# Row order for the later batches' scores, and the second batch's loads queued behind the second weight quarter

## The chip, the cores and the metric

One core of one Trainium2 chip runs the whole program. The metric is the device time of one execution in microseconds (us). Before the change it is 761.84 us, the median of 3 runs (760.61 to 761.95).

## The reference

Four batches (B) of 576 rows (S) go through attention with 8 heads (H) of 64 numbers (D), whose keys and values are first condensed to 32 memory slots (M), and then through two feed-forward layers of 512 and 2048 columns. Everything is float32.

```python
a = softmax(phi, axis=sequence)                      # b h s m
k_m, v_m = a.T @ k, a.T @ v                          # b h 32 64
attn = softmax(q @ k_m.T / 8, axis=memory) @ v_m     # b h 576 64
x = attn.transpose(0, 2, 1, 3).reshape(2304, 512)
x = lrelu(x @ w_in) @ w_out                          # first layer, slope 0.01
h = x @ w_in2
out = (h * tanh(softplus(h))) @ w_out2               # second layer, result 2304 x 512
```

## The kernel before, in words

The kernel has one TensorE (PE), VectorE (DVE) and ScalarE (ACT), and one queue (SP) that issues every DMA in program order. Attention and the first layer are joined: with `win` (a quarter of `w_in`, 512 columns) the condensed values are multiplied ahead (`vw_tasks`, L923: the product at L943, then a high and a low part of it in 32-bit rounded form by `hi_lo`, L317), so that a row of softmax weights (`at_t`) times `vw_t` gives the hidden layer (`stage1`, L1182: product at L1193, evictions at L1207, difference at L1214, second product with `wo_t` at L1226). The work of `stage1` comes in items of one batch, one half of its 576 rows (288 columns of the moving operand) and one 128-column block `m` of the hidden layer. The first 16 items are those of batch 0: 8 with the first quarter of `w_in`, 8 with the second; then follows batch 1. The weights come as bit patterns of float64 and are decoded by ACT and DVE (`load_raw`, L342; `decode`, L359); the first two quarters go through seven raw buffers, `raw_t` (3) and `raws_t` (4).

For batches 1 to 3, `kv_rest` (L502) loads phi, k and v and condenses them (fold at L522, PE at L533, L557, L597, the condensing product at L620, transposes at L651 to L663), and `score_rest` (L674) loads q, transposes it in 32 x 32 blocks on DVE (L691), so that a partition holds one number of a head's 32 and the free dimension holds (r, e, i) for row 18 i + r and half e of the 64, and multiplies it with the keys on PE (L709), in two halves of the rows. A half has 2 x 4 x 2 products; each stands in the trace as two PE instructions, so a half is 32. Softmax follows on DVE and ACT (L720 to L752). Half `hf` takes the rows with r from 9 hf to 9 hf + 8, and its 288 columns stand in the order (r, i).

Two other lines that the prediction uses: the reductions of phi in batch 0 (L450) read it in steps of 32 elements, where those of the scores (L729) read neighbours; batch 0's copies of the transposed q (L840, recorded as L310) write it in steps of 9 elements.

The second layer works on blocks of 768 rows. Its last products (`chunk`, L1617: product L1701, evictions at L1729 and L1736) end in result tiles of 128 rows and 256 columns, which `fo` (L1743) stores. Because of the order of the columns, a result tile's 128 partitions are rows at one distance (2) only in batch 0, whose q goes another way (`score_tasks`, L807); in the later batches they are 4 (or 3, 2, 1) groups of 32 rows, each row 18 from the next.

The order on each engine is written by a planner (`Order.run`, L94) when the program is built. Every task has a due time (`prio`), costs and dependencies; among those ready by the planner's own clock the earliest due is issued. The loads of batch 1 are due by `pl` and `pq`; the second half of its scores by `S1` after the first. Buffers come from small rings; two PSUM tiles `misc_t` serve L533 to L663, L709 and L943 in turn.

Of the kernel before, what the change touches and what calls it, by code (L numbers as in the profile page):

```python
# [23 lines left out]
def hop(a, b):  # L24
# [4 lines left out]


K = dict(
    LAG1=2, WIN=8, OB=2, RS=4, FILL=36, A1=10, S1=2.8,
    A2=30, S2=2.6, V1=2.4, V2=14, W2=56.0, W2S=3.8, O='phi0 kv0 phi1 q0 w0 kv1 q1 w1 w2 w3', HF0=-20.0, HF1=-7.0,
    HFD=0.3, TOP=0.3, HI=0.2, WO=2.0, WOL=1, WC=3.0, WC0=-38.0, V0=3.0, COLD=20, GL=1.5, AL=5.0, XL=22.0, T='0:1 0:1 1:2 0:2 1:2', SB=1,
    DW=280e3, DQ=1.3, DP=1.2, DS=0.78, DI=0.38, L4=0.5, L4P=1.6, L4S=0.8, L4T=5.0, MA=6, QL=4, FK=-52.5, DWF=0.85, MV="......rvvrrvvrvr",
)


# [35 lines left out]
class Task:  # L74
    def __init__(self, engines, prio, fn, deps, take, use, bias):
        self.engines, self.prio, self.fn, self.take = engines, prio, fn, take
        self.deps = [d for d in deps if d is not None]
        self.after, self.end, self.bias = [], None, bias
        for b in list(take) + list(use):
            b.users.append(self)  # L80


class Order:
# [10 lines left out]
    def run(self, window):  # L94
        n_wait, ready = {}, []
        for i, t in enumerate(self.tasks):
            t.n = i
            t.deps = list({id(d): d for d in t.deps + [d for b in t.take for d in b.res.after]}.values())
            n_wait[i] = len(t.deps)
            for d in t.deps:  # L100
                d.after.append(t)
            if not t.deps:
                t.at = dict.fromkeys(t.engines, 0.0)
                ready.append(t)
        free = {"PE": 1.7, "ACT": 1.5, "DVE": 0.5, "POOL": 0.8, "SP": 0.0}
        events = []
        now, dma_free, left, main = 0.0, 1.68, len(self.tasks), -1.0
        while left:
            ready.sort(key=lambda t: (t.prio, t.n))
            hit = False  # L110
            for t in list(ready):
                if t.prio > main + window and t.take:
                    continue
                start = {e: max(now, free[e], t.at[e]) for e in t.engines}
                eng = min(start, key=lambda e: start[e] + t.engines[e] + t.bias.get(e, 0))
                if start[eng] > now + 1e-9:
                    continue
                got = []
                for b in t.take:
                    if not b.res.can_take(b, now, eng):  # L120
                        break
                    b.res.take(b)
                    got.append(b)
                if len(got) < len(t.take):
                    for b in got:
                        b.res.undo()
                    continue
                t.eng, t.st0 = eng, now
                self.issued = 0
                t.fn(eng)  # L130
                if eng == "SP":
                    free[eng] = now + K["DI"] * self.issued
                    dma_free = max(dma_free, now + 0.6) + t.engines[eng]
                    t.end = dma_free + 1.8
                else:
                    free[eng] = t.end = now + t.engines[eng]
                main = max(main, getattr(t, "main", -1.0))
                ready.remove(t)
                left -= 1
                hit = True  # L140
                for a in t.after:
                    n_wait[a.n] -= 1
                    if not n_wait[a.n]:
                        a.at = {e: max(d.end + hop(d.eng, e) for d in a.deps) for e in a.engines}
                        ready.append(a)
                        for x in a.at.values():
                            heapq.heappush(events, x)
                for e in free:
                    heapq.heappush(events, t.end + hop(eng, e))
                heapq.heappush(events, free[eng])  # L150
            if not hit:
                while events and events[0] <= now:
                    heapq.heappop(events)
                assert events, [(t.prio, t.fn.__qualname__) for t in ready[:12]]
                now = events[0]
        return now
# [3 lines left out]
def kernel(  # L160
# [341 lines left out]
    def kv_rest(b, p0, dp):  # L502
        ph = tags["phi"].new([P, HG, RB, M])
        kv = [kvq.new([P, 2, 2, RB, D]) for _ in range(NG)]
        pl = p0 - 6
        pairs = lambda x: x[b].rearrange("(x e) (t j) d -> (e t) x j d", e=2, j=RB)
        l_phi = load(pl, ph.make, lambda: pairs(phi), 589824, (), [ph], (), K["DS"])

# [1 line left out]
        for g in range(NG):  # L510

            def ld(e, g=g):
                kv[g].make()
                for j, x in enumerate((k, v)):
                    dma(out=kv[g].t[:, j], in_=pairs(x)[:, 2 * g:2 * g + 2])

            l_kv.append(add({"SP": K["DS"] * mb(1179648)}, pl + 0.2 + 0.1 * g, ld, (), [kv[g]]))

        def fold(buf, op, last):
            xs = ph.t.rearrange("p x j m -> p j x m")  # L520
# [153 lines left out]
    def score_rest(b, pq, ps, dp):  # L674
# [3 lines left out]
        for g in range(NG):  # L678
            flat = lambda g=g: q_of[g]().rearrange("p r e i -> p (r e i)")
            new = b == 1 or not g  # L680

            def ld(e, g=g, new=new, flat=flat):
                if new:
                    qs[g].make()
                dma(out=flat(), in_=q[b, g * HG:(g + 1) * HG].rearrange("h (p r) d -> (h p) (r d)", r=RQ))

            ld0 = add(
                {"SP": K["DS"] * mb(589824)}, pq - K["QL"], ld, [] if new else [ld0], [qs[g]] if new else [], [] if new else [qs[g]],
            )
            parts.append(add(  # L690
                {"DVE": dve(1152) + 0.1}, pq + 0.7 * g, lambda e, flat=flat: nc.vector.transpose(out=flat(), in_=flat()), [ld0], (), [qs[g]],  # L691
            ))
# [3 lines left out]
        for hf in range(2):  # L696
# [4 lines left out]
            def fsc(e, hf=hf, T=T, pss=pss):  # L701
                T.make()
                for x in pss:
                    x.make()
                for y in range(2):
                    for h in range(HG):
                        for g in range(NG):
                            rows, o = slice(M * h, M * (h + 1)), M * (h ^ g)
                            nc.tensor.matmul(  # L709
                                out=pss[g].t[o:o + M, :].rearrange("p (r i) -> p r i", i=M),  # L710
                                lhsT=kb.t[rows, g, y, :],
                                rhs=q_of[g]()[rows, RB * hf:RB * (hf + 1), y, :],
                                start=(y == 0),
                                stop=(y == 1),
                            )
# [202 lines left out]
            [] if hf else [a], [T, a] if hf else [T],  # L918
        )))

    win, win_ready, w_scr = {}, {}, {}

    def vw_tasks(b, c, p0):  # L923

# [70 lines left out]
    def w_chunk(c):  # L995
        p = at_item["1", 0, 0, 4 * c] - K["WC"] if c else K["WC0"]
        for g in range(NG):
            wb = win_tag.new([P, 2, 512])
            win[0, c, g] = wb
            ready = []  # L1000
            for j in range(2):
                b, ld = load_raw(p - K["WOL"] + 0.1 * j if c else PW[2 * g + j], "w", 2 * g + j, c, raws if c < 2 else rawm)
                ready.append(
                    decode(
                        p + 0.1 * (2 * g + j), b, ld, (lambda wb=wb, j=j: wb.t[:, j]),
                        ready[:1], [wb] if j == 0 else [], [] if j == 0 else [wb],
                    )
                )
            win_ready[0, c, g] = ready

            def f(e, c=c, g=g, wb=wb):
                d = dram.tile([P, 2, 512], F32, name=f"wscr{c}{g}")
                w_scr[c, g][0] = d
                dma(out=d, in_=wb.t)

            w_scr[c, g] = [None, None]
            w_scr[c, g][1] = add({"SP": mb(524288)}, p + 3, f, ready, (), [wb])
# [580 lines left out]

    out_v = out.rearrange("(b p r) f -> b r p f", b=B, r=2)
    out_b = [out_v[x // 2, x % 2] for x in range(2 * B)]  # L1600
    out_j = [out[x // 2 * S:(x // 2 + 1) * S].rearrange("(i u j) f -> u j i f", u=2, j=RB)[x % 2] for x in range(2 * B)]
    rows = [(ob_tag.new([P, DM]), 0) for _ in range(2)]
    for j in range(2):
        xo = x1_tag.slots[j].new([P, 2 * S])
# [12 lines left out]
    def chunk(c):  # L1617
# [10 lines left out]
        for k7, (nm, a, tn, way) in enumerate(PROD):  # L1628
# [91 lines left out]
            for t in range(NT):  # L1720
# [20 lines left out]
                if half2 and nm in ("P4", "P5", "P2", "P3"):  # L1741

                    def fo(e, g=g, t=t, k2=k2, ob=ob):  # L1743
                        x = (2 * s + g) * NB2 + t * P
                        end = x + P
                        while x < end:
                            hf, p0 = divmod(x, NB1)
                            n = min(NB1 - p0, end - x)
                            o = x - (end - P)
                            cs = slice(k2 * 256, (k2 + 1) * 256)  # L1750
                            if hf < 2:
                                dma(out=out_b[hf][p0:p0 + n, cs], in_=ob.ap()[o:o + n, :])
                            else:
                                dma(out=out_j[hf][p0 // M:(p0 + n) // M, :, cs], in_=ob.ap()[o:o + n, :])
                            x += n

                    add({"SP": mb(P * 1024)}, pe_p + 0.1, fo, [ev], (), [ob])
# [55 lines left out]
```

## Time and profile before

| | us |
|---|---|
| median of 3 runs | 761.84 |
| the profiled execution | 761.22 |
| its span | 759.3 |
| PE busy in the span | 733.2 (97%) |
| DVE busy | 545.0 (72%) |
| ACT busy | 404.0 (53%) |

The chain of waits that ended last is PE for 92% of the span, and its two largest lines are L1226 (27%) and L1547 (21%). PE's granted clock is 0.99 of full speed as a mean. Rows in a profile name line, engine, operation and output<-inputs; "x" is a count, and "idle before" is the time for which the engine stood still ahead of an instruction, with what released it. Where many instructions of PE run side by side, their durations overlap, so a stretch's length says more than their sum.

### The profile page before, as it was taken

The page shows a single profiled execution, that of the slowest core. Times are in us where ns is not written, and L with a number is a line of the kernel's source. Part 1 is how long each engine was busy: PE and PEld are TensorE (multiplying, and loading weights), DVE is VectorE, ACT ScalarE, POOL GpSimd, SP SyncE. Part 2 cuts the span into 40 slices and gives each one's busy share as a digit, 9 for nine tenths or more (in the row PEclk, how much of TensorE's full clock was granted, in tenths as well). Part 3 has the DMA queues.
Part 4 walks back from the last instruction along what each step waited for, and adds up shares of the span by engine and source line. Part 5 has one row for each costly group of instructions (what it writes and reads, how often), then busy time and mean ns, then how long its engine had stood idle before and what let it go on. Part 6 is the DMA issues. An engine that isn't in the chain of part 4 may idle for free.

```text
span 759.3 us, 16148 instructions
## 1 busy us (share of the span) xinstructions
PE 733.2 (97%) x6167; PEld 700.9 (92%) x6167; DVE 545.0 (72%) x1137; ACT 404.0 (53%) x883; POOL 0.7 (0%) x6
## 2 busy tenths in 40 slices
PE   8898999999999999999999999999999999999992
PEld 7685999988998989999999999999999999999992
DVE  6897759787676957465779898675677856656781
ACT  3865449545464556464466656544555644454440
POOL 0000000000000000000000000000000000000000
PEclk9999999999999999999999999999999999999997
DMA  9952955547858397864279888788988788895572
GB/s 349 412 203 85 343 174 185 190 143 267 279 198 328 128 316 270 269 225 149 88 284 380 304 318 264 243 250 283 293 262 252 231 263 257 274 297 165 158 229 70
DMA packets 90274, 183.76 MB, mean 242 GB/s; under 512 B 7510, under 2 KB 42326, under 8 KB 90198
## 3 DMA queue, kind: packets, MB, share of 16 engines
q1 hardware_dynamic: 90198, 182.74, 71.4%
q8 instruction: 48, 0.79, 0.4%
q14 instruction: 28, 0.23, 0.1%
HBM read 140.25 MB, written 42.47 MB: 241 GB/s over the span
## 4 chain that ended last, share of the span: by engine, by line
PE 92%; DVE 2%; DMA 2%; ACT 1%; issue 1%; SPq 0%; DVEq 0%; ACTq 0%
PE acc_t L1226 27%; PE h_t L1547 21%; PE acc_t L1701 16%; PE h_t L1193 13%; PE misc_t L1701 6%; PE acc_t L1547 2%; PE misc_t L943 2%; PE misc_t L620 1%; DMA kvq_t<-in_q_dram 1%; PE acc_t L484 1%; DMA wo_t<-tscr 1%; PE misc_t L709 1%; PE acc_t L1024 1%; PE h_t L833 0%; DVE raws_t L387 0%
## 5 line engine op out<-in xcount | busy, mean ns | idle before, releaser
L1226 PE MATMUL acc_t<-hi_t,wo_t 128*128 128x288 f32 x1024 | 161.5, 298 | 0.4 <-ACT at_t L310 0.3
L1226 PEld LDWEIGHTS acc_t<-hi_t,wo_t 128*128 128x128 f32 x1024 | 143.7, 188 | 10.3 <-issue 4.7
L1701 PE MATMUL acc_t<-wo_t,hi_t 128*128 128x256 f32 x720 | 134.1, 280 | 1.3 <-DMA wo_t<-tscr 1.3
L1193 PE MATMUL h_t<-at_t,vw_t 128*128 128x288 f32 x768 | 124.4, 298 | 2.2 <-ACT at_t L310 0.8
L1701 PEld LDWEIGHTS acc_t<-wo_t,hi_t 128*128 128x128 f32 x720 | 118.1, 188 | 2.1 <-issue 1.0
L1207 ACT ACTIVATE hi_t<-h_t 128x288 fp32r<-128x288 f32 x128 | 52.6, 411 | 119.7 <-PE acc_t L1226 102.9
L1193 PEld LDWEIGHTS h_t<-at_t,vw_t 128*128 128x128 f32 x768 | 110.0, 190 | 3.2 <-ACT at_t L310 1.1
L1701 PE MATMUL acc_t<-wo_t,lo_t 128*128 128x256 f32 x360 | 102.1, 284 | 0.0
L1214 DVE TENSOR_TENSOR lo_t<-e_t,hi_t 128x288 fp32r<-128x288 f32 x128 | 57.2, 450 | 54.0 <-ACT e_t L1207 26.4
L1226 PE MATMUL acc_t<-lo_t,wo_t 128*128 128x288 f32 x512 | 90.6, 299 | 1.4 <-DVE lo_t L1214 1.4
L1226 PEld LDWEIGHTS acc_t<-lo_t,wo_t 128*128 128x128 f32 x512 | 74.6, 188 | 8.7 <-issue 6.2
L1547 PE MATMUL h_t<-xt_t,vw_t 128*128 128x384 f32 x396 | 79.1, 336 | 0.0
L1670 DVE TENSOR_TENSOR lo_t<-wo_t,hi_t 128x384 fp32r<-128x384 f32 x94 | 52.0, 555 | 37.2 <-ACT hi_t L310 35.8
L1547 PE MATMUL h_t<-xt_t,wo_t 128*128 128x384 f32 x352 | 75.5, 336 | 0.0
L1701 PEld LDWEIGHTS acc_t<-wo_t,lo_t 128*128 128x128 f32 x360 | 67.7, 188 | 0.0
L1547 PEld LDWEIGHTS h_t<-xt_t,vw_t 128*128 128x128 f32 x396 | 66.7, 188 | 0.3 <-DVE wo_t L1566 0.3
L310 ACT ACTIVATE hi_t<-wo_t 128x384 fp32r<-128x384 f32 x83 | 43.4, 523 | 41.3 <-PE acc_t L1701 28.8
L1547 PEld LDWEIGHTS h_t<-xt_t,wo_t 128*128 128x128 f32 x352 | 59.5, 188 | 0.1
L1701 PE MATMUL misc_t<-wo_t,hi_t 128*128 128x256 f32 x288 | 54.1, 280 | 0.0
L1207 ACT ACTIVATE e_t<-h_t 128x288 f32<-128x288 f32 x128 | 52.0, 406 | 0.0
L1670 DVE TENSOR_TENSOR lo_t<-vw_t,hi_t 128x384 fp32r<-128x384 f32 x50 | 27.7, 555 | 25.5 <-ACT hi_t L310 25.2
L1572 ACT ACTIVATE wo_t<-wo_t 128x384 f32<-128x384 f32 x53 | 27.6, 520 | 32.4 <-DVE wo_t L1566 32.2
(242 smaller groups left out, 1050.9 us busy)
## 6 DMA issues: line engine op xcount, KB each, us to landing
wo_t<-tscr SPq DMA_DIRECT2D x168, 256.0 KB
vw_t<-wsum SPq DMA_DIRECT2D x32, 512.0 KB
win_t<-wscr SPq DMA_DIRECT2D x24, 512.0 KB
raw_t<-in_moe_w_in_dram SPq DMA_DIRECT2D x19, 512.0 KB
raw_t<-in_moe_w_out_dram SPq DMA_DIRECT2D x17, 512.0 KB
wsum<-vw_t SPq DMA_DIRECT2D x16, 512.0 KB
wo_t<-wsum SPq DMA_DIRECT2D x16, 512.0 KB
tscr<-raw_t SPq DMA_DIRECT2D x9, 512.0 KB
```

The lines of the kernel that those rows point to most:

```text
L310: nc.scalar.activation(out=o, in_=i, func=AF.Copy)
L484: nc.tensor.matmul(out=acc.t[rows, :].rearrange("p (j d) -> p j d", j=2), lhsT=phv()[rows, r, :], rhs=kv.t[rows, :2304].rearrange("p (j r ...
L620: nc.tensor.matmul(out=accs_[g].t[o:o + M, :].rearrange("p (j d) -> p j d", j=2), lhsT=ph.t[rows, x, j, :], rhs=kv[g].t[rows, :, x % 2, j, :],
L943: nc.tensor.matmul(out=pss[g].t[M * (h ^ g):M * (h ^ g) + M, :], lhsT=vT[b, g][0].t[rows, g, h ^ g if b else h // 2, :], rhs=wbs[g].t[rows ...
L1193: nc.tensor.matmul(out=h.t, lhsT=us[g][0].t[:, wi, j0:j0 + P], rhs=ats[g][0].t[:, ai, cols], start=(n == 0), stop=(n == 3 * NG - 1),)
L1207: nc.scalar.activation(out=o, in_=h.t, func=AF.Prelu, alpha=0.01)
L1214: lambda e: nc.vector.tensor_tensor(out=lb.make(), in0=eb.t, in1=hb.t.bitcast(F32), op=ALU.subtract),
L1226: nc.tensor.matmul(out=ac[kk].t, lhsT=wu[0].t[:, wi, kk * P:(kk + 1) * P], rhs=(hb if src == 0 else lb).t, start=(first and (wi, src) == ( ...
L1547: nc.tensor.matmul(out=h.t, lhsT=w[:, wi, c0:c0 + P], rhs=xp[b, xi].ap()[:, j], start=(first and j == 0 and k3 == 0), stop=(j == 1 and k3 ...
L1572: lambda e: nc.scalar.activation(out=t_of[x](), in_=h.t if h else t_of[x](), func=AF.Mish),
L1670: lambda e, hb=hb, lb=lb, src=src: nc.vector.tensor_tensor(out=lb.make(), in0=src(), in1=hb.t.bitcast(F32), op=ALU.subtract),
L1701: nc.tensor.matmul(out=ac[t].t, lhsT=x.t[:, t * P:(t + 1) * P], rhs=T[:, wi], start=(u == 0 and n3 == 0 and first_of), stop=(u == CH - 1 a ...
```

## The change

Four things change. The column order of the scores of batches 1 to 3 becomes (i, r) with r of one parity per half, so that column c of half u is row 2 c + u. For this PE reads q at L709 in steps of 128 elements (512 bytes) instead of one after the other. Second, all result tiles are stored by the one form that batch 0 had, 128 rows at distance 2. Third, a task can name loads that must have been issued ahead of it (`behind`): batch 1's k, v and q wait for the fourth load of the second quarter of `w_in` (index 3 of `w_loads[1]`; index 9 is beyond the list and asks nothing of phi). Fourth, `S1` goes from 2.8 to 8.0, which puts the second half of batch 1's scores later.

```diff
-    LAG1=2, WIN=8, OB=2, RS=4, FILL=36, A1=10, S1=2.8,
+    LAG1=2, WIN=8, OB=2, RS=4, FILL=36, A1=10, S1=8.0,
-    ... MA=6, QL=4, FK=-52.5, ...
+    ... MA=6, QL=4, PL=6, BH=(9,3,3,3,3), FK=-52.5, ...
...
-        self.after, self.end, self.bias = [], None, bias
+        self.after, self.end, self.bias, self.behind = [], None, bias, []
...
-                if t.prio > main + window and t.take:
+                if t.prio > main + window and t.take or any(not hasattr(x, "st0") for x in t.behind):
...
-        pl = p0 - 6
+        pl = p0 - (K["PL"] if b == 1 else 6)
...
+        if b == 1:
+            l_phi.behind, l_kv[0].behind, l_kv[1].behind = [w_loads[1][x:x + 1] for x in K["BH"][:3]]
...
+            if b == 1:
+                ld0.behind = w_loads[1][K["BH"][3 + g]:][:1]
...
-                                out=pss[g].t[o:o + M, :].rearrange("p (r i) -> p r i", i=M),
+                                out=pss[g].t[o:o + M, :].rearrange("p (i r) -> p i r", i=M),
                                 lhsT=kb.t[rows, g, y, :],
-                                rhs=q_of[g]()[rows, RB * hf:RB * (hf + 1), y, :],
+                                rhs=q_of[g]()[rows].rearrange("p (r u) e i -> p u e i r", u=2)[:, hf, y],
...
+                w_loads[c].append(ld)
...
-    out_j = [out[x // 2 * S:(x // 2 + 1) * S].rearrange("(i u j) f -> u j i f", u=2, j=RB)[x % 2] for x in range(2 * B)]
...
-                            if hf < 2:
-                                dma(out=out_b[hf][p0:p0 + n, cs], in_=ob.ap()[o:o + n, :])
-                            else:
-                                dma(out=out_j[hf][p0 // M:(p0 + n) // M, :, cs], in_=ob.ap()[o:o + n, :])
+                            dma(out=out_b[hf][p0:p0 + n, k2 * 256:(k2 + 1) * 256], in_=ob.ap()[o:o + n, :])
```

What the planner makes of it shows at three places. On SP near the start (`wscr` is a quarter of `w_in` written back after decoding, `in_moe_w_in_dram` a load of `w_in`, here of its second quarter), before:

```order
L279 DMA kvq_t<-in_k_dram 128x2x576
L279 DMA kvq_t<-in_v_dram 128x2x576
L279 DMA wscr_369<-win_t 128x1024
L279 DMA raw_t<-in_moe_w_in_dram 128x1024
L279 DMA qs_t<-in_q_dram 128x1152
L279 DMA raw_t<-in_moe_w_in_dram 128x1024
L279 DMA kvq_t<-in_k_dram 128x2x576
L279 DMA kvq_t<-in_v_dram 128x2x576
L279 DMA qT_t<-in_q_dram 128x1152
L279 DMA wscr_458<-win_t 128x1024
L279 DMA raws_t<-in_moe_w_in_dram 128x1024 x2
L279 DMA raws_t<-in_moe_w_out_dram 128x1024 x2
```

And the same place of the changed kernel:

```order
L279 DMA wscr_366<-win_t 128x1024
L279 DMA raw_t<-in_moe_w_in_dram 128x1024 x2
L279 DMA wscr_448<-win_t 128x1024
L279 DMA raws_t<-in_moe_w_in_dram 128x1024 x2
L279 DMA kvq_t<-in_k_dram 128x2x576
L279 DMA kvq_t<-in_v_dram 128x2x576
L279 DMA kvq_t<-in_k_dram 128x2x576
L279 DMA kvq_t<-in_v_dram 128x2x576
L279 DMA qs_t<-in_q_dram 128x1152
L279 DMA qT_t<-in_q_dram 128x1152
L279 DMA raws_t<-in_moe_w_out_dram 128x1024 x2
```

All six loads of batch 1's k, v and q moved behind the four loads of the second quarter. On PE, in batch 0's second half of `stage1`, before:

```order
L1226 MATMUL acc_t<-hi_t,wo_t 128x288 x8
L1226 MATMUL acc_t<-lo_t,wo_t 128x288 x4
L1226 MATMUL acc_t<-hi_t,wo_t 128x288 x8
L1226 MATMUL acc_t<-lo_t,wo_t 128x288 x4
L1226 MATMUL acc_t<-hi_t,wo_t 128x288 x8
L597 MATMUL misc_t<-ones,rm_t 128x1 x2
L1226 MATMUL acc_t<-lo_t,wo_t 128x288 x4
L943 MATMUL misc_t<-win_t,vTb_t 32x512 x8
L620 MATMUL misc_t<-kvq_t,phi_t 32x128 x72
L1193 MATMUL h_t<-at_t,vw_t 128x288 x12
```

In the changed kernel (its L947 is L943 of before, L1231 is L1226, L1198 is L1193, L535 is L533, L559 is L557), some 15 rows earlier:

```order
L1231 MATMUL acc_t<-lo_t,wo_t 128x288 x4
L947 MATMUL misc_t<-win_t,vTb_t 32x512 x8
L1231 MATMUL acc_t<-hi_t,wo_t 128x288 x8
L1198 MATMUL h_t<-at_t,vw_t 128x288 x6
L1231 MATMUL acc_t<-lo_t,wo_t 128x288 x4
L535 MATMUL misc_t<-ident,rm_t 128x128
L1198 MATMUL h_t<-at_t,vw_t 128x288 x6
L1231 MATMUL acc_t<-hi_t,wo_t 128x288 x6
L559 MATMUL misc_t<-rm_t,ones 64x128 x2
L1231 MATMUL acc_t<-hi_t,wo_t 128x288 x2
L1231 MATMUL acc_t<-lo_t,wo_t 128x288 x4
L1231 MATMUL acc_t<-hi_t,wo_t 128x288 x8
```

The product with the second quarter (L943) moved ahead of batch 1's three small PE steps, and `stage1`'s first products go on without a break; L620 stands 20 rows behind L943 now. On SP at the end of the program, a piece of the difference:

```order
-L279 DMA out_dram<-ob_t 4x32x256
-L279 DMA out_dram<-ob_t 2x32x256 x2
-L279 DMA out_dram<-x_t 4x32x256
-L279 DMA out_dram<-ob_t 4x32x256
-L279 DMA out_dram<-ob_t 2x32x256 x2
-L279 DMA out_dram<-x_t 4x32x256
+L279 DMA out_dram<-ob_t 128x256
+L279 DMA out_dram<-ob_t 64x256 x2
+L279 DMA out_dram<-x_t 128x256
+L279 DMA out_dram<-ob_t 128x256
+L279 DMA out_dram<-ob_t 64x256 x2
+L279 DMA out_dram<-x_t 128x256
```

Only the form of the stores changed there, not their number or place. Behind the second half of batch 1's scores the rows of PE are the same in both kernels.

## Rows read from the trace of the kernel before

**Rows 1.** Busy time by stretch: us, PE, PEld, DVE, ACT, POOL, clock, DMA share, GB/s.

```profile
46.00:58.00 12.00, 11.70 (x97) 10.27 (x95) 10.94 (x23) 8.12 (x20) 0.00 (x0) 1.00 0.23 90
58.00:66.00 8.00, 4.82 (x154) 3.78 (x147) 6.19 (x12) 5.02 (x10) 0.00 (x0) 0.79 0.55 188
...
80.00:200.00 120.00, 120.00 (x1124) 110.05 (x1123) 87.72 (x186) 66.11 (x156) 0.00 (x0) 1.00 0.66 229
...
380.00:735.00 355.00, 354.42 (x2509) 353.44 (x2508) 260.76 (x538) 188.90 (x393) 0.00 (x0) 1.00 0.81 264
```

**Rows 2.** Chain that ended last, its end: start, us, what.

```profile
737.81 6.88 DMA wo_t<-tscr
...
746.24 0.35 DVE x_t L1736
```

**Rows 3.** Busy time by stretch, one full stretch and the end.

```profile
536.00:541.00 5.00, 5.00 (x39) 5.00 (x38) 4.12 (x9) 2.18 (x5) 0.00 (x0) 1.00 1.01 337
...
746.00:748.00 2.00, 0.13 (x2) 0.00 (x0) 0.59 (x2) 0.00 (x0) 0.00 (x0) 1.00 0.25 80
...
756.00:758.00 2.00, 0.00 (x0) 0.00 (x0) 0.00 (x0) 0.00 (x0) 0.00 (x0) 0.50 0.12 44
```

**Rows 4.** DMA issues on SP in order of time: start, us.

```profile
536.89 0.34 SPq L279 DMA_DIRECT2D out_dram<-ob_t  x1
...
746.41 3.86 SPq L279 DMA_DIRECT2D out_dram<-ob_t  x3
750.37 1.14 SPq L279 DMA_DIRECT2D out_dram<-x_t  x1
```

**Rows 5.** Waits of SP from 730 us on: us, times, longest.

```profile
SPq L1808 <- DMA out_dram<-ob_t: 5.4, 1, 5.4
...
SPq L1808 <- DMA out_dram<-x_t: 1.3, 1, 1.3
```

**Rows 6.** Waits of PE in the whole span.

```profile
PE misc_t L620 <- DVE vw_t L326: 2.5, 2, 2.4
...
PE acc_t L1701 <- DMA wo_t<-tscr: 1.3, 3, 0.7
```

**Rows 7.** SP and DVE from 31 to 57 us, in order of time.

```profile
31.12 4.54 SPq L279 DMA_DIRECT2D raws_t<-in_moe_w_in_dram  x2
...
34.60 0.68 DVE L326 TENSOR_TENSOR wo_t<-raws_t,wo_t 128x512 fp32r<-128x512 f32 x1
...
56.28 0.68 DVE L387 SCALAR_TENSOR_TENSOR win_t<-raws_t 128x512 int32<-128x512 int32 x1
```

**Rows 8.** L620 from 55 to 70 us, and from 220 to 250 us: busy, mean ns.

```profile
L620 PE MATMUL misc_t<-kvq_t,phi_t 64*32 64x128 f32 x144 | 4.4, 396 | 3.2 <-DVE vw_t L326 2.5 <-issue 0.7
...
L620 PE MATMUL misc_t<-kvq_t,phi_t 64*32 64x128 f32 x144 | 2.2, 271 | 0.0
```

**Rows 9.** SP and DVE at the start, in order of time.

```profile
0.74 0.40 SPq L279 DMA_DIRECT2D phi_t<-in_phi_dram  x1
...
3.78 1.14 DVE L450 TENSOR_REDUCE rm_t<-phi_t 128x32 f32<-128x576 f32 x1 [2.82 <-DMA phi_t<-in_phi_dram]
```

**Rows 10.** Chain that ended last: one half of batch 3's scores.

```profile
245.27 1.13 PE misc_t L709 x32
```

**Rows 11.** PE in order of time: two neighbouring rounds of batch 1's scores.

```profile
69.64 0.40 PE L709 MATMUL misc_t<-qs_t,kT_t 32*32 32x288 f32 x1
...
69.88 0.40 PE L709 MATMUL misc_t<-qs_t,kT_t 32*32 32x288 f32 x1
```

**Rows 12.** DVE and ACT by line and form: busy, mean ns.

```profile
L450 DVE TENSOR_REDUCE rm_t<-phi_t 128x32 f32<-128x576 f32 x4 | 4.5, 1131 | 3.8 <-DMA phi_t<-in_phi_dram 2.8 <-ACT phi_t L466 1.0
L729 DVE TENSOR_REDUCE sm_t<-T_t 128x18 f32<-128x576 f32 x2 | 1.5, 749 | 0.0
...
L310 ACT ACTIVATE kvq_t<-h_t 128x384 f32<-128x384 f32 x2 | 1.7, 861 | 3.6 <-PE h_t L833 3.6
```

**Rows 13.** The page's groups of instructions: busy, mean ns of one.

```profile
L310 ACT ACTIVATE hi_t<-wo_t 128x384 fp32r<-128x384 f32 x83 | 43.4, 523 | 41.3 <-PE acc_t L1701 28.8
```

More of the change, by code (lines that the diff above doesn't have):

```diff
@@ L31 @@
 K = dict(
-    LAG1=2, WIN=8, OB=2, RS=4, FILL=36, A1=10, S1=2.8,
+    LAG1=2, WIN=8, OB=2, RS=4, FILL=36, A1=10, S1=8.0,
     A2=30, S2=2.6, V1=2.4, V2=14, W2=56.0, W2S=3.8, O='phi0 kv0 phi1 q0 w0 kv1 q1 w1 w2 w3', HF0=-20.0, HF1=-7.0,
     HFD=0.3, TOP=0.3, HI=0.2, WO=2.0, WOL=1, WC=3.0, WC0=-38.0, V0=3.0, COLD=20, GL=1.5, AL=5.0, XL=22.0, T='0:1 0:1 1:2 0:2 1:2', SB=1,
-    DW=280e3, DQ=1.3, DP=1.2, DS=0.78, DI=0.38, L4=0.5, L4P=1.6, L4S=0.8, L4T=5.0, MA=6, QL=4, FK=-52.5, DWF=0.85, MV="......rvvrrvvrvr",
+    DW=280e3, DQ=1.3, DP=1.2, DS=0.78, DI=0.38, L4=0.5, L4P=1.6, L4S=0.8, L4T=5.0, MA=6, QL=4, PL=6, BH=(9,3,3,3,3), FK=-52.5, DWF=0.85, MV="......rvvrrvvrvr",
 )
@@ L919, in half @@
         )))
-    win, win_ready, w_scr = {}, {}, {}
+    win, win_ready, w_scr, w_loads = {}, {}, {}, [[] for _ in range(NC)]
     def vw_tasks(b, c, p0):
@@ L1749, in fo @@
                             o = x - (end - P)
-                            cs = slice(k2 * 256, (k2 + 1) * 256)
-                            if hf < 2:
-                                dma(out=out_b[hf][p0:p0 + n, cs], in_=ob.ap()[o:o + n, :])
-                            else:
-                                dma(out=out_j[hf][p0 // M:(p0 + n) // M, :, cs], in_=ob.ap()[o:o + n, :])
+                            dma(out=out_b[hf][p0:p0 + n, k2 * 256:(k2 + 1) * 256], in_=ob.ap()[o:o + n, :])
                             x += n
```

## The prediction

> **What bounds the kernel now.** I read the page's busy times first: PE is the bound. The table of stretches says where it is not full: between 80 and 200 us PE is busy for all of 120 us and from 380 to 735 us for 354.4 of 355, while DVE stands at about 73% [rows 1]. In such a stretch a PE instruction more or less is time more or less, and nothing else is. So I looked for what lies outside: the start, the stretch around 60 us, and the end.
>
> At the end the last additions on DVE finish at 746.24 + 0.35 = 746.6 us [rows 2], but the span ends at 759.3 us, 12.7 us later. In this time no engine works, and the DMA share is 0.25, then 0.12: with 16 DMA engines, 4 and then 2 of them [rows 3]. In the stretch 536 to 541 us, where batch 0's tiles are stored among weight loads, the share was 1.01 at 337 GB/s against 80 and 44 GB/s here [rows 3]. So the last stores are spread over 4 and 2 engines: the 4x32x256 and 2x32x256 forms of the order have an outermost size of 4 and 2. SP has issued its last store at 750.37 + 1.14 = 751.5 us [rows 4], then waits 5.4 and 1.3 us for stores to land [rows 5], which makes 758.2 us; 1.1 us of closing follow. The same stores stood ahead of a weight load: the chain has 6.88 us in `wo_t<-tscr` at 737.81 us [rows 2], and PE waited 1.3 us in three pieces for such loads [rows 6].
>
> In the stretch 58 to 66 us PE works for 4.82 of 8 us at a mean clock of 0.79 [rows 1]. It has come to the end of what the first weight quarter allows: the last decoding of the second quarter is at 56.28 us [rows 7], L943 follows, and L620 waits 2.5 us for DVE to read the two `misc_t` [rows 6]. [...]
>
> **The change part by part.**
>
> *Stores.* No store is added or taken away, only their form changes. In the new form 128 partitions are the outermost size, as in batch 0, whose store was issued in 0.34 us [rows 4]. The end then comes out as follows: last addition 746.6; issue to landing 3.0 us, by the first load of the program, which was issued at 0.74 and used at 3.78 us and is 295 KB where the last stores are 64 to 128 KB [rows 9]; closing 1.1. That is 750.7. The two last groups of stores are 768 KB, at 337 GB/s 2.3 us of transfer, issued over 6 us, so they don't queue. The 1.3 us for which PE waited for weight loads go as well, since the load at 737.81 us stands behind short transfers. 749.4 instead of 759.3: **-9.9 us**. [...] The stores in the middle of the layer change nothing, since PE is full there [rows 1].
>
> *Loads.* The four loads of the second quarter lie ahead of 3.5 MB of k, v and q (4 x 0.59 + 2 x 0.59). The last of them waits for its buffer: the second issue of the pair that starts at 31.12 us ends at 35.66 [rows 7], since its raw buffer holds a block of `w_out` that DVE reads at 34.60 to 35.28 us [rows 7]. That wait stays. So three of the four come early, the fourth at about 37 to 38 us, where decoding it (two passes on ACT, one on DVE, some 0.7 us each) can be over by about 46 us instead of 57, as the new order places it between `stage1`'s evictions. L943 stands there, at some 46.5 us, and `stage1` goes on. What is gained is what PE loses from 46 to 66 us: 0.3 us of idle in the first stretch, 8 - 4.82 = 3.2 in the second [rows 1], and 4.4 - 2.2 = 2.2 for the clock [rows 8], together 5.7. What is late next: batch 1's loads are now queued on SP behind that fourth load. 0.5 + 3.5 MB from 35.7 us at 0.4 MB/us (0.34 MB/us in the full stretch [rows 3], and this stretch has nothing beside it) land at 46 to 49 us, a few us after they are used by DVE (46.4 us) today, but the new order has put those transposes behind the decoding; L620 needs them at about 59 us. Behind them the `w_out` blocks of the second quarter come at about 50 us, for use at about 60. Between L943 and L620 five tenants share the two `misc_t` in turn, with DVE between any two. I leave 0.7 us for waits of this kind: **-5.0 us**. Bounds: -5.7, and 0 (L620 waits as long as now, and the clock falls again).
>
> *Second half of the scores, later.* It moves 32 instructions by some 10 us. DVE is the engine that gets room by it (10.9 of 12 us busy from 46 to 58 us [rows 1]); the half is needed only 8 items later. No cost, covered by these 8 items of `stage1`, some 20 us; without this cover PE would wait for softmax, at most as long as DVE's work on one half, some 5 us.
>
> *Scores in steps.* Six halves of L709 (three batches), each 1.13 us on the path [rows 10]. Eight instructions run side by side; a round of them takes 0.24 us [rows 11], 0.83 ns a column, and a half has four rounds. Now q is read in steps of 128 elements. No row shows PE reading so. Bounds: nothing (the same instructions and columns; I exclude a gain, since neighbours are the easiest case in every row), and what DVE and ACT pay for steps. DVE's reduction of 576 in steps takes 1131 ns against 749 [rows 12], 0.66 ns an element more. ACT's copy of 384 with stepped writes takes 861 ns [rows 12] against 523 [rows 13], 0.88 ns more. For PE that is 288 x 4 x 0.66 = 0.76 us a half or 1.01. I take the DVE row, a read like PE's: 6 x 0.76 = **+4.6 us**, upper bound +6.1, all on the path (batches 2 and 3 in full stretches, batch 1 once its gap is gone). [...]
>
> **Sum.** From the profiled execution, 761.2 (span 759.3): 761.2 - 9.9 - 5.0 + 4.6 = 750.9. This execution lies 0.6 us below the median of the runs, so I say 751.
>
> **The rivals.**
>
> *A. Steps are free for PE.* [...] Then 761.2 - 14.9 = 746.3.
>
> *B. The second quarter comes early, but another wait takes the gap's place:* DVE is busy for 10.9 of 12 us from 46 to 58 us [rows 1], and decoding, L691, L565 and the fold all stand ahead of L597 and L620. For it: the same two `misc_t`. Against it: 20 rows of `stage1` now lie between. Then the loads give nothing: 761.2 - 9.9 + 4.6 = 755.9.
>
> [...]
>
> *D. The stores don't spread:* stepped rows in memory still go by few engines, or memory takes them no faster. Then the end stays, 761.2 - 5.0 + 4.6 = 760.8. Against it stands batch 0's form in the full stretch [rows 3].
>
> **How the numbers follow.** Forecast 0.48 (its own range 748.5 to 753), A 0.30, B 0.12, C 0.05, D 0.05. A measurement of this kernel can tell 0.2%, 1.5 us, from no change. Faster: the forecast, A and B, and a little of D, 0.91. Same: most of D, 0.04. Slower: C, 0.05. The range that leaves out no more than 2 in 10: from A with a little more at the end, 744.5, to B, 756.
>
> **What would show it.** At the end: a DMA share near 1 in short bursts instead of 0.25, no long wait of SP after its last issue, and 3 to 5 us from the last addition to the end of the span instead of 12.7. Near 60 us: L943 at about 46 us, no idle time of PE over 1 us between 46 and 70, a clock of 1.00, and L620 at 2.2 us. At L709: rounds of 0.24 us (A), 0.43 to 0.5 (forecast) or near 1 (C). The prediction is wrong if the end still takes over 9 us, or if L620 has its wait back, or if L709's half is above 2.6 us more.

## The result and the profile after

The changed kernel takes 751.45 us, the median of 4 runs (751.03 to 752.24), against 761.23 (759.55 to 761.95, 4 runs) for the kernel before: a ratio of 0.9876, 95% interval 0.9856 to 0.9896, so 1.2% faster. The forecast was 751.0. The profiled execution took 751.76 us with a span of 749.9, so it is 9.4 us of span that have to be found. In the changed kernel's listing L713 is L709 of before, L622 is L620, L947 is L943, L1198 and L1231 are L1193 and L1226, L1219 is L1214, L1705 and L1740 are L1701 and L1736, L724 is L720.

**The end.** The chain of waits still ends with DVE's last addition, and SP's last issues follow it.

```profile
745.63 0.35 DVE x_t L1740
```

```profile
745.29 1.54 SPq L279 DMA_DIRECT2D out_dram<-ob_t  x3
746.93 0.54 SPq L279 DMA_DIRECT2D out_dram<-x_t  x1
```

Waits of SP from 730 us on (us, times, longest), the two that stood in [rows 5]:

```profile
SPq L1808 <- DMA out_dram<-ob_t: 0.9, 1, 0.9
...
SPq L1808 <- DMA out_dram<-x_t: 0.5, 1, 0.5
```

The last addition ends at 745.98 instead of 746.6 us [rows 2], and the span 3.9 us later instead of 12.7. The issues became shorter too (three in 1.54 us against 3.86, one in 0.54 against 1.14 [rows 4]), and SP's waits of 5.4 and 1.3 us [rows 5] are 0.9 and 0.5. Busy time by stretch, with the columns of [rows 1], first for two microseconds and then for the busiest half of one:

```profile
746.00:748.00 2.00, 0.00 (x0) 0.00 (x0) 0.00 (x0) 0.00 (x0) 0.00 (x0) 1.00 0.45 134
```

```profile
748.00:748.50 0.50, 0.00 (x0) 0.00 (x0) 0.00 (x0) 0.00 (x0) 0.00 (x0) 1.00 0.72 250
```

A share of 0.72 is 11 or 12 of the 16 DMA engines, where 4 and 2 worked before [rows 3]. The share near 1 that the prediction named as a sign did not come.

PE waits for no load of `wo_t` in L1705 any more (1.3 us before [rows 6]). Those waits cost more than they show, because the profile counts idle time from an instruction's recorded end, and the recorded durations overlap. In the kernel before:

```profile
741.10 0.28 PE L1701 MATMUL acc_t<-wo_t,lo_t 128*128 128x256 f32 x1
742.11 0.48 PE L1701 MATMUL acc_t<-wo_t,hi_t 128*128 128x256 f32 x2 [0.73 <-DMA wo_t<-tscr]
```

Undisturbed, these instructions start 0.12 us after each other, so this stop cost 1.01 - 0.12 = 0.89 us where 0.73 is shown; the three cost 1.8 us, and 2.0 with the two products behind each, which take 0.31 us instead of 0.24.

**The stretch around 60 us.** Busy time by stretch, with the columns of [rows 1]:

```profile
46.00:58.00 12.00, 12.00 (x99) 11.64 (x92) 11.20 (x23) 8.28 (x19) 0.00 (x0) 1.00 0.79 302
58.00:66.00 8.00, 7.00 (x180) 6.03 (x179) 7.32 (x20) 6.56 (x16) 0.00 (x0) 1.00 0.23 66
```

PE works for 7.00 of the 8 us that had 4.82 [rows 1], at a clock of 1.00 where 0.79 stood. That mean came from these six microseconds of the kernel before:

```profile
60.00:62.00 2.00, 1.24 (x40) 0.97 (x48) 2.00 (x5) 2.00 (x4) 0.00 (x0) 0.77 0.89 262
62.00:64.00 2.00, 2.00 (x94) 2.00 (x82) 1.97 (x5) 0.91 (x2) 0.00 (x0) 0.50 0.41 164
64.00:66.00 2.00, 1.35 (x42) 0.81 (x27) 0.33 (x1) 0.11 (x1) 0.00 (x0) 0.88 0.00 0
```

In order of time on PE, the product with the second quarter, and L622 between 55 and 70 us:

```profile
45.01 1.09 PE L947 MATMUL misc_t<-win_t,vTb_t 64*32 64x512 f32 x16
```

```profile
L622 PE MATMUL misc_t<-kvq_t,phi_t 64*32 64x128 f32 x144 | 2.6, 272 | 1.0 <-issue 1.0
```

L622's mean is 272 ns, that of a later batch in [rows 8], and its wait for DVE is gone. The 1.0 us of idle that is left in it has no releaser in the profile ("issue"); it stands on the edge of the prediction's sign, no idle time over 1 us. On SP the second quarter's last load is issued, and batch 1's loads right behind it, in the changed kernel:

```profile
26.41 7.64 SPq L279 DMA_DIRECT2D raws_t<-in_moe_w_in_dram  x2
34.10 0.43 SPq L279 DMA_DIRECT2D kvq_t<-in_k_dram  x1
```

**The scores.** Pieces of the chain of waits, one half of batch 1 and one of batch 2 (the count of the second is short of records):

```profile
66.45 2.09 PE misc_t L713 x32
...
155.01 2.57 PE misc_t L713 x23
```

Both were 1.13 us before, as the half in [rows 10]. So steps cost 2 x (2.09 - 1.13) in batch 1 and, with 2.57 and 2.56 for the two halves, 4 x 1.435 in batches 2 and 3: 1.9 + 5.7 = 7.7 us. The forecast had 4.6 and an upper bound of 6.1.

The traces close the sum. Batch 2's L622 is one point on the chain, the last addition another:

```profile
144.05 2.18 PE misc_t L620 x144
```

```profile
139.70 2.18 PE misc_t L622 x144
```

Ahead of the first point 4.35 us are gained although batch 1's steps cost 1.9: the front gives 6.3. From there to the last addition the kernel before takes 602.54 us and the changed one 606.28, 3.7 more where steps alone would be 5.7: the stops for weight loads give 2.0. With the drain's 8.8 that is -6.3 - 2.0 - 8.8 + 7.7 = -9.4, the whole difference of the spans.

### The profile page after: what moved, and what is told of

The parts are those of the page before. It is cut to its first block, busy times and chain, and to the rows that moved or that the text cites. A ratio compares the mean times of both kernels' runs of the same rounds, so it can differ in the third digit from the quotient of the medians.

```text
span 749.9 us, 16151 instructions
## 1 busy us (share of the span) xinstructions
PE 737.7 (98%) x6167; PEld 699.1 (93%) x6167; DVE 546.1 (73%) x1138; ACT 404.2 (54%) x882; POOL 0.7 (0%) x6
## 4 chain that ended last, share of the span: by engine, by line
PE 96%; DVE 1%; DMA 1%; ACT 1%; issue 0%; SPq 0%
PE acc_t L1231 28%; PE h_t L1552 22%; PE acc_t L1705 17%; PE h_t L1198 13%; PE misc_t L1705 7%; PE misc_t L947 2%; PE acc_t L1552 2%; PE misc_t L713 2%; PE acc_t L484 1%; PE misc_t L622 1%; DMA kvq_t<-in_q_dram 1%; PE acc_t L1029 1%; PE h_t L837 0%; PE misc_t L864 0%; PE misc_t L665 0%
## 5 line engine op out<-in xcount | busy, mean ns | idle before, releaser
L1231 PE MATMUL acc_t<-hi_t,wo_t 128*128 128x288 f32 x1024 | 160.9, 298 | 0.4 <-ACT at_t L310 0.3
L1231 PEld LDWEIGHTS acc_t<-hi_t,wo_t 128*128 128x128 f32 x1024 | 143.5, 188 | 12.5 <-issue 6.7
L1705 PE MATMUL acc_t<-wo_t,hi_t 128*128 128x256 f32 x720 | 133.8, 279 | 0.0
L1198 PE MATMUL h_t<-at_t,vw_t 128*128 128x288 f32 x768 | 124.6, 297 | 2.2 <-ACT at_t L310 0.8
L1705 PEld LDWEIGHTS acc_t<-wo_t,hi_t 128*128 128x128 f32 x720 | 118.1, 188 | 0.2 <-DVE ob_t L312 0.2
L1198 PEld LDWEIGHTS h_t<-at_t,vw_t 128*128 128x128 f32 x768 | 110.1, 190 | 3.1 <-ACT at_t L310 1.1
L1705 PE MATMUL acc_t<-wo_t,lo_t 128*128 128x256 f32 x360 | 102.1, 284 | 0.0
L1219 DVE TENSOR_TENSOR lo_t<-e_t,hi_t 128x288 fp32r<-128x288 f32 x128 | 57.5, 451 | 47.9 <-ACT e_t L1212 23.8
L1231 PE MATMUL acc_t<-lo_t,wo_t 128*128 128x288 f32 x512 | 90.6, 299 | 1.0 <-DVE lo_t L1219 1.0
L1231 PEld LDWEIGHTS acc_t<-lo_t,wo_t 128*128 128x128 f32 x512 | 74.6, 188 | 10.6 <-issue 8.6
L1705 PEld LDWEIGHTS acc_t<-wo_t,lo_t 128*128 128x128 f32 x360 | 67.6, 188 | 0.0
L1705 PE MATMUL misc_t<-wo_t,hi_t 128*128 128x256 f32 x288 | 54.0, 279 | 0.0
```

What stands on the lines that cost most here:

```text
L1198: nc.tensor.matmul(out=h.t, lhsT=us[g][0].t[:, wi, j0:j0 + P], rhs=ats[g][0].t[:, ai, cols], start=(n == 0), stop=(n == 3 * NG - 1),)
L1219: lambda e: nc.vector.tensor_tensor(out=lb.make(), in0=eb.t, in1=hb.t.bitcast(F32), op=ALU.subtract),
L1231: nc.tensor.matmul(out=ac[kk].t, lhsT=wu[0].t[:, wi, kk * P:(kk + 1) * P], rhs=(hb if src == 0 else lb).t, start=(first and (wi, src) == ( ...
L1705: nc.tensor.matmul(out=ac[t].t, lhsT=x.t[:, t * P:(t + 1) * P], rhs=T[:, wi], start=(u == 0 and n3 == 0 and first_of), stop=(u == CH - 1 a ...
```

## Experiments

Each time stands beside runs of the kernel before on the same chip (medians 759.2 to 760.5 us in the four groups of runs); the ratio carries the verdict.

### One part at a time

**Stores alone**, in the kernel before:

```diff
-                            if hf < 2: ... out_b ... else: ... out_j ...
+                            dma(out=out_b[hf][p0:p0 + n, k2 * 256:(k2 + 1) * 256], in_=ob.ap()[o:o + n, :])
```

Expected: 

> The kernel before with the stores of the changed kernel and nothing else (the columns stay in the old order, so result rows of the later three batches are put at exchanged places). Theory: the form of the stores alone is worth what the two traces show at the end, the drain from the last addition to the end of the span 12.7 to 4.0 us (-8.7), and about 2 us of PE's waits for late weight loads in the last 30 us: 761.2 - 10.7 = 750.5. My forecast's term of 9.9 would give 751.3. Rival: part of the short drain comes from the changed start (other order on the queue), then the drain stays above 6 us and the time above 754.

Measured: 751.67 us against 760.22, ratio 0.9871 (0.9843 to 0.9900), so 7.6 to 11.9 us of gain. DVE at the end of its trace:

```profile
745.66 0.42 DVE L1736 TENSOR_TENSOR x_t<-x_t,acc_t 128x256 f32<-128x256 f32 x1
```

The last addition ends at 746.1 and the span at 750.0: 3.9 us, as in the changed kernel. The store form alone makes the short drain; the rival falls. From batch 2's L620 (145.53 us here) to the last addition it takes 600.55 us, 2.0 less than before, as in the changed kernel.

**Loads and S1 alone**, in the kernel before (its reads and stores kept):

```diff
+PL=6, BH=(9,3,3,3,3), S1=8.0   (and the code of `behind`)
```

Expected: 

> The kernel before with the order of the loads (the lists of loads to wait for, and S1 at 8.0) and nothing else. Theory from the two traces: batch 2's first L620 starts 4.35 us earlier although batch 1's scores cost 1.9 us more, so the loads are worth 6.3: 761.2 - 6.3 = 754.9. By the forecast's term of 5.0: 756.2. Rival: the gap at 58 to 66 us would have gone without L943 at 45 us; then less than 3 us, above 758.

Measured: 753.8 us, ratio 0.9909 (0.9892 to 0.9925): 5.7 to 8.2 us of gain. Batch 2's L620 on the chain measures the front, since PE's work ahead of it is the same; in the kernel before it starts at 144.05 us (above), here at

```profile
137.99 2.18 PE misc_t L622 x144
```

6.06 us earlier. Not all of this is the change. A row ahead of the stretch, in the kernel before and then here (in brackets the idle time and its releaser):

```profile
40.34 0.79 PE L1226 MATMUL acc_t<-lo_t,wo_t 128*128 128x288 f32 x4 [1.08 <-DVE lo_t L1214]
```

```profile
39.77 0.79 PE L1231 MATMUL acc_t<-lo_t,wo_t 128*128 128x288 f32 x4 [0.23 <-DVE lo_t L1219]
```

In the profiled executions this row starts between 38.7 and 40.3 us with the front of before and between 38.4 and 40.4 with the new one, so the 0.57 us ahead of it says nothing. Behind it 5.5 us are gained: the 5.7 of my stretch less the one new wait here, 0.2 us in L622. In the changed kernel, which has the row at 38.72 us and 1.0 us of such a wait, it is 4.65 without the steps.

That the times say 5.7 to 8.2 has a likely source in the same wait. With the front of before its size differs between executions: 0.65 us in the kernel before, 2.8 with both halves undone (below), and with the stores alone

```profile
65.34 0.61 PE L620 MATMUL misc_t<-kvq_t,phi_t 64*32 64x128 f32 x10 [2.51 <-issue]
```

With the new front it is 0 to 1.0 us. The prediction has no term for it, and what PE waits for there stays open.

**Steps alone**, in the kernel before:

```diff
-out=pss[g].t[o:o + M, :].rearrange("p (r i) -> p r i", i=M)
+out=pss[g].t[o:o + M, :].rearrange("p (i r) -> p i r", i=M)
-rhs=q_of[g]()[rows, RB * hf:RB * (hf + 1), y, :]
+rhs=q_of[g]()[rows].rearrange("p (r u) e i -> p u e i r", u=2)[:, hf, y]
```

Expected: 

> The kernel before with q read in steps of 128 elements and nothing else (its result rows of the later three batches are put at exchanged places). Theory from the traces: a half of batches 2 and 3 grows from 1.13 to 2.57 us, four times 1.44, and batch 1's scores by 1.9: 761.2 + 7.7 = 768.9. By the forecast's term of 4.6: 765.8. Rival A (steps are free for PE, the longer rounds in the trace are the instructions' overlap as modelled): 761.2. In batch 1, whose scores stand in a gap here, the cost may be partly hidden: then 767.

Measured: 766.8 us, ratio 1.0079 (1.0059 to 1.0099), 4.5 to 7.5 us slower. Its halves on the chain are 2.09 in batch 1 and 2.57 in batch 2:

```profile
68.57 2.09 PE misc_t L709 x32
...
160.44 2.57 PE misc_t L709 x23
```

Steps are not free: rival A falls. Batch 1's cost is not hidden behind the gap. From its first half to batch 2's L620 the kernel before takes 144.05 - 69.44 = 74.61 us and this run 145.12 - 68.57 = 76.55, 1.94 more, which is 2 x (2.09 - 1.13):

```profile
69.44 1.13 PE misc_t L709 x32
```

```profile
145.12 2.18 PE misc_t L620 x144
```

What is missing of the 7.7 lies at the start (the first half comes 0.87 us earlier here) and behind the scores (the drain takes 11.9 us here instead of 12.7).

**The changed kernel with neighbours** (the same four lines taken back):

Expected: 

> The changed kernel with q read as neighbours again and nothing else taken back (its result rows of the later three batches are put at exchanged places). Theory: the whole cost of the steps comes back, 751.4 - 7.7 = 743.8. By the forecast's term of 4.6: 746.8. Rival A, steps free: 751.4.

Measured: 743.07 us, ratio 0.9770 (0.9753 to 0.9786); the changed kernel without the steps is 8.4 us faster than with them, against 7.7 from the chain's pieces; the two medians come from different groups of runs (8.1 by the ratios). Every half is 1.13 us again:

```profile
65.22 1.13 PE misc_t L713 x32
...
151.86 1.13 PE misc_t L713 x32
```

### What a step costs PE

**Steps of 2 and of 4**, in the changed kernel (w is 2, or 4):

```diff
+out=pss[g].t[o:o + M, :].rearrange("p (w r i) -> p w r i", w=w, r=RB)
+rhs=q_of[g]()[rows, RB * hf:RB * (hf + 1), y, :].rearrange("p r (i w) -> p w r i", w=w)
```

Expected, steps of 2: 

> The changed kernel with q read in steps of 2 elements (8 bytes; the 16 even i of each r, then the odd ones) instead of 128 (its result rows of the later three batches are put at exchanged places). The whole cost of the steps is 751.4 - 743.1 = 8.3 us. [...] Any step costs the same: 0.64 and 751.4. Only far steps cost: 0.24 and 743.

Expected, steps of 4: 

> As the run in steps of 2, with steps of 4 elements (16 bytes; its result rows of the later three batches are put at exchanged places). [...] Only far steps cost: 743.

Measured: 744.65 us, ratio 0.9801 (0.9769 to 0.9833), and 749.33 us, ratio 0.9862 (0.983 to 0.9895). One half of batch 1 and one of batch 2, in steps of 2:

```profile
67.81 1.14 PE misc_t L713 x32
...
154.51 1.14 PE misc_t L713 x32
```

And in steps of 4:

```profile
66.63 2.08 PE misc_t L713 x32
...
155.19 2.12 PE misc_t L713 x30
```

By these halves a step of 8 bytes is free. (The time is 1.6 us above that with neighbours, but from batch 2's L622 to the end of the span, where four of the six halves lie, the two profiles have 604.4 and 604.5 us.) A step of 16 bytes costs in batch 1 what 512 bytes cost, 2.08 against 2.09 us. So the number is neither "any step" nor "far steps". In steps of 512 bytes a column takes 1.67 ns (the four rounds of a half last 2.09 us, 0.48 us between starts, for 288 columns each), where neighbours take 0.83 [rows 11]; steps of 16 bytes have the half of the first, 2.08 us, and steps of 8 bytes that of the second, 1.14 us against 1.13. No step between 8 and 16 bytes was run, and no row shows what in PE's reading makes the difference.

**The dearer halves of batches 2 and 3.** There both groups of heads (g) lie in one tile, 4608 bytes apart, which is 9 x 512; batch 1 has two tiles, whose distance no row shows. Groups of instructions of L713 in the changed kernel (nanoseconds: lowest, median, highest), batch 1 and then batch 2:

```profile
L713 PE MATMUL misc_t<-qs_t,kT_t x16: 648/658/660, 66.4 to 67.9; 32*32 32x288 f32 x16
```

```profile
L713 PE MATMUL misc_t<-kvq_t,kT_t x32: 732/777/804, 154.9 to 156.8; 32*32 32x288 f32 x32
```

The edit takes the other half of e for the second group, so that the reads side by side are 128 bytes off that distance:

```diff
-lhsT=kb.t[rows, g, y, :], rhs=...[:, hf, y]
+lhsT=kb.t[rows, g, y ^ g, :], rhs=...[:, hf, y ^ g]
```

Expected: 

> The changed kernel with the two halves of a head's 64 numbers (e) taken in the other order for the second group of four heads: two reads side by side in one partition then lie 32 elements (128 bytes) off the distance that is a multiple of 512 bytes. Theory that the 0.64 us of a round in batches 2 and 3 (batch 1, from two tiles: 0.48) come from that distance: rounds of 0.48, 4 halves x 4 x 0.16 = 2.6 us less, 748.9. Rival (the distance is nothing to it): rounds as before, 751.4.

Measured: 749.96 us, ratio 0.9871 (0.9837 to 0.9904), and batch 2 now reads as batch 1 does:

```profile
L713 PE MATMUL misc_t<-kvq_t,kT_t x32: 648/658/660, 154.2 to 155.7; 32*32 32x288 f32 x32
```

So the distance of the two streams was the further cost, by 4 x (2.57 - 2.08) = 1.9 us on the chain; my 2.6 had 0.16 us a round, where it is 0.12. The time alone could not show it: its two executions, 748.97 and 750.95 us, lie too far apart.

**Steps of 64:**

```diff
+rhs=q_of[g]()[rows, RB * hf:RB * (hf + 1), y, :].rearrange("p r i -> p i r")
```

Expected: 

> The changed kernel with q read in steps of 64 elements (256 bytes) instead of 128 (a half has neighbouring r instead of every second; result rows of the later three batches are put at exchanged places). [...] For the further cost in batches 2 and 3 (2.57 against 2.09 a half): if two streams at 4608 bytes collide only where the steps of both are multiples of 512 bytes, 2.09 there too and 749.4; if steps of 256 bytes collide as well, 2.57 and 751.4.

Measured: 750.85 us, ratio 0.9889 (0.9853 to 0.9924), and on the chain

```profile
65.75 2.09 PE misc_t L713 x32
...
154.33 2.57 PE misc_t L713 x22
```

At 4608 bytes apart, steps of 256 bytes take 2.57 us a half as those of 512 do, while steps of 16 bytes take 2.12. The runs have only this distance and the one 128 bytes off it.

### The front: loads and S1 taken apart

These three runs, and the last one, start from a kernel with the new stores and with the order (i, r) made behind softmax instead of on PE (its edit stands further down; 743.03 us).

**S1 back at 2.8:**

Expected: 

> The run with the order mended later, with S1 back at 2.8: the second half of batch 1's scores follows the first at once, as in the kernel before, while the order of the loads stays. My step said that the later place costs and brings nothing: then 743.0 within 1.5. Rival: DVE has no room for a second softmax there (11.3 of 12 us busy from 46 to 58 us, 7.2 of 8 from 58 to 66 in the run with neighbours), and PE waits for its evictions: 745 or more.

**Loads not behind** (`BH=(9,9,9,9,9)`, S1 at 8.0):

Expected: 

> The run with the order mended later, with batch 1's k, v and q free to go ahead of the second weight quarter again, as in the kernel before, and S1 left at 8.0. Theory that the loads' order carries the whole gain of the front: 743.0 + 6.4 = 749.4, with L620 waiting for DVE some 2.4 us and a clock below 0.9 or an idle PE between 58 and 66 us. Rival: the later second half carries part of it, then below 748.

**Both:**

Expected: 

> The run with the order mended later, with both halves of the front undone: the loads free as before and S1 back at 2.8. With one of the two undone the time was 749.9 (S1) and 749.5 (loads) against 743.0 with both. Theory that each is worth nothing without the other: 750 again (748.5 to 751.5; the kernel before with the new stores alone, whose front and PE reads are the same, had 751.7). Rival that each is worth its 6.5 by itself: 756.

| loads | S1 | us | ratio to before | batch 2's L622 on the chain |
|---|---|---|---|---|
| behind | 8.0 | 743.03 | 0.9784 (0.9759 to 0.9809) | 136.56 |
| behind | 2.8 | 749.94 | 0.9880 (0.9853 to 0.9908) | 143.24 |
| free | 8.0 | 749.48 | 0.9874 (0.9847 to 0.9901) | 142.58 |
| free | 2.8 | 750.89 | 0.9879 (0.9854 to 0.9903) | 145.48 |

Neither edit is by itself worth anything that these times can tell; together they are worth 7.9 us (7.2 by the ratios; the four rows come from three groups of runs). (L622 in the profiled executions comes 2.2 and 2.9 us earlier with one of them, and 8.9 with both.) This is the miss of the study, mine before the change and in the first of the three expectations. With S1 at 2.8 the stretch around 60 us is mended, and the gap comes back at 76 us. PE's largest wait, then the stretches, then the chain that ended last:

```profile
PE acc_t L1231 <- DVE x_t L1276: 2.5, 3, 1.8
```

```profile
58.00:64.00 6.00, 6.00 (x175) 5.47 (x176) 5.90 (x16) 5.83 (x15) 0.00 (x0) 1.00 0.17 63
...
76.00:82.00 6.00, 3.48 (x14) 2.47 (x13) 5.93 (x14) 0.96 (x2) 0.00 (x0) 0.77 0.94 305
82.00:88.00 6.00, 6.00 (x33) 6.00 (x33) 1.77 (x4) 1.18 (x4) 0.00 (x0) 0.67 1.04 410
...
84.00:85.00 1.00, 1.00 (x6) 1.00 (x5) 0.00 (x0) 0.00 (x0) 0.00 (x0) 0.50 1.02 411
```

```profile
72.06 0.66 DVE T_t L753
72.72 0.07 DVE T_t L737
...
78.01 0.66 DVE T_t L753
...
79.03 0.68 DVE T_t L756
79.72 0.35 DVE x_t L1276
...
80.11 4.42 PE acc_t L1231 x16
```

The chain leaves PE and runs through DVE. On DVE the second half's softmax (L737 at 72.72, L753 at 78.01, L756 at 79.03) stands in one queue with the last steps of the first half and with the additions L1276 that `stage1`'s products wait for. PE idles for 2.5 us from 76 to 82. The granted clock is 1.00 up to 79 us, 0.50 from 80 to 86 and 1.00 again behind that, which makes the means of 0.77 and 0.67: 16 products of L1231 take 4.42 us, where the chain of the run with S1 at 8.0 has 20 of them in 2.63:

```profile
82.72 2.63 PE acc_t L1231 x20
```

With the loads free and S1 late, the gap is the old one (stretches, then L622 between 52 and 66 us):

```profile
52.00:58.00 6.00, 4.36 (x41) 3.20 (x39) 5.62 (x16) 4.85 (x11) 0.00 (x0) 1.00 0.27 98
58.00:64.00 6.00, 4.63 (x146) 3.88 (x147) 4.71 (x9) 3.54 (x7) 0.00 (x0) 0.72 0.50 167
```

```profile
L622 PE MATMUL misc_t<-kvq_t,phi_t 64*32 64x128 f32 x144 | 4.3, 391 | 2.7 <-DVE vw_t L326 2.5 <-issue 0.2
```

With both edits PE is full from 40 to 200 us, the stretch that broke in the run with S1 at 2.8 among them:

```profile
76.00:82.00 6.00, 6.00 (x54) 5.00 (x53) 5.86 (x14) 2.59 (x6) 0.00 (x0) 1.00 0.98 333
```

### A version that beats both

PE reads runs of 32 neighbours, and the copy to the high part and the subtraction of the low part change the order:

```diff
+rhs=q_of[g]()[rows].rearrange("p (r u) e i -> p u e r i", u=2)[:, hf, y]     (out as "p r i")
+hi and lo = a[g].t[:, x, cols].rearrange("p (i r) -> p i r", r=RB)
+src       = T.t[:, g].rearrange("p r i -> p i r")
```

Expected: 

> The changed kernel, but PE reads q in runs of 32 neighbours (every second r of 32 i), and the order (i, r) is made two steps later: the copy of the softmax weights to their high part and the subtraction of the low part read their 288 columns in steps of 32 elements. The result is the reference's. Theory (it is PE's path that makes the steps dear): the 24 stepped instructions cost DVE and ACT about 288 x 0.66 ns = 0.19 us each, 4.6 us in all, beside a PE that is full, so the time is that of the run with neighbours, 743 (742 to 745). Rival: softmax is waited for, and the 4.6 us come back on the path, 747.7.

Measured: 743.03 us (742.6 to 744.37), ratio 0.9784 (0.9759 to 0.9809), the time of the run with neighbours. DVE and ACT pay for the steps; the run with neighbours first, then this one:

```profile
L326 DVE TENSOR_TENSOR at_t<-T_t,at_t 128x288 fp32r<-128x288 f32 x16 | 6.6, 451 | 0.1
L310 ACT ACTIVATE at_t<-T_t 128x288 fp32r<-128x288 f32 x12 | 5.0, 443 | 4.2 <-DVE T_t L756 3.8 <-DVE T_t L912 0.3
```

```profile
L326 DVE TENSOR_TENSOR at_t<-T_t,at_t 128x288 fp32r<-128x288 f32 x16 | 9.4, 625 | 0.1
L310 ACT ACTIVATE at_t<-T_t 128x288 fp32r<-128x288 f32 x12 | 7.6, 669 | 4.7 <-DVE T_t L756 4.4 <-DVE T_t L912 0.3
```

2.8 us more on DVE and 2.6 on ACT (and 0.3 in the four copies that DVE makes), where 4.6 were expected, and nothing on the end: PE is what the time goes by, so the same reordering is free here one engine further on, 743.03 us against 743.07 with neighbours.

## Why the prediction came out, and where it was wrong

- *Stores, -9.9.* Right in mechanism, a little too small: 10.8 in the traces. The drain is 3.9 us where the sum had 3.0 + 1.1 from the addition on; PE's waits cost 2.0 us and not the 1.3 that is shown as idle. The stores alone measured 7.6 to 11.9.
- *Loads, -5.0.* Right in mechanism. Behind the row at 40 us the size is right too: 4.65 us in the changed kernel, whose new wait is 1.0 us where 0.7 had been set aside, and 5.5 with the loads alone. But by the times they are worth 5.7 to 8.2, at or beyond the bound of 5.7, and the likely rest, the wait without a releaser in L620 (0.65 us in the profile that I read, up to 2.8 in others), was in no term.
- *"Second half of the scores, later. No cost, covered by these 8 items".* The step that failed, though not by its own number. That it costs nothing held; that the front's gain belongs to the loads alone did not. Without it the gain is gone, because DVE's queue then breaks PE's run 15 us later (2.5 us of idle from 76 to 82 us) and the clock falls again (0.50 from 80 to 86). The view was there: DVE at 10.9 of 12 us [rows 1]. The only price that I gave, 5 us, was for a half that comes too late; for one that comes too early there was none, and it is 6.9 (749.94 against 743.03): 2.5 us of idle, and by an estimate from the two stretches 6 x 0.23 + 6 x 0.33 = 3.4 for the clock.
- *Steps, +4.6.* The right sign, mis-sized: 7.7 by the chain, 8.4 by removing them. DVE's 0.66 ns a column more was the nearest row, but PE pays 0.84 (1.67 instead of 0.83) in batch 1, and 1.25 ((2.57 - 1.13) / 1152) in batches 2 and 3, whose two groups lie 4608 bytes apart. The second cost was in no term and no bound.
- *The sum.* The parts were -9.9 - 5.0 + 4.6 = -10.3 and are -10.8 - 6.3 + 7.7 = -9.4. Steps that are 3.1 dearer stand against 0.9 more on the stores and 1.3 more at the front, and of the front's 6.3 there are 1.6 us ahead of the row at 40 us, where executions differ anyway. That the forecast of 751 met 751.45 so closely is luck.
- *The rivals.* A (746.3) falls by the runs with steps alone and with neighbours, C, the slower case, by halves of 2.09 and 2.57 us, which is 0.48 and some 0.6 for a round where it had near 1. D falls by the store run. B did not happen, but it is what the loads without S1 do: another DVE wait takes the gap's place, only at 76 us.

## What to carry to other kernels

When a gap on the bounding engine is closed, look for the next place where the engine that feeds it is full: two edits can each be worth nothing and together the whole gap, so undo them one by one and both. Put a reordering on the engine with idle time: here 24 stepped instructions on DVE and ACT were free (743.03 us against 743.07) and 192 on PE cost 8 us. The stores whose outermost size is 128 instead of 4 or 2 were issued here in under half the time (three in 1.54 us against 3.86, one in 0.54 against 1.14) and had 0.72 of the DMA engines busy in the best half microsecond of the end, where it had been 0.25 and 0.12, which counts where nothing is left to hide it.

## What the runs showed of the hardware that was not expected

- PE's float32 reads in steps of 8 bytes cost nothing (1.14 us a half, 1.13 with neighbours), in steps of 16 bytes in batch 1 as much as in steps of 512 (2.08 and 2.09).
- Two groups of products that read the same partitions side by side, 4608 bytes apart, in steps of 256 or 512 bytes, take 2.57 us a half, where batch 1 takes 2.09; 128 bytes off that distance, in steps of 512, 2.08.
- An idle time of PE of 2.5 us in all from 76 to 82 us was followed by a granted clock of 0.50 up to 86 us, so that 16 products took 4.42 us.
- Three stops of PE that show as 1.3 us of idle made the stretch 2.0 us longer.
